# Query products with the masked kv in two 64-feature row tiles, for three of four head groups

## The chip, the cores and the metric

The kernel runs on one core of a Trainium2 chip. The metric is the device time of the whole program in microseconds (us); for the kernel before it is 183.64 us, the median of three runs (183.57 to 183.75). The engines are named as in the profile: PE is TensorE's matmul stream and PEld its weight loads, DVE is VectorE, ACT is ScalarE, POOL is GpSimd, SP is SyncE, which issues most DMAs.

## What is computed

Two blocks read the same layer-normed input of 2048 rows by 512 and are summed with it: a linear attention of 32 heads of 16 features ("A"), and a dense layer with a mish-like activation ("B", 512 to 1792 and back).

```python
def _A_ref(x, wqkv, w_phi, wo):          # x is layer-normed
    q, k, v = heads of x @ wqkv           # 32 heads of 16
    pq, pk = q @ w_phi[h], k @ w_phi[h]
    phi_q = concat([softmax(pq), softmax(-pq)])   # 32 features a head
    phi_k = concat([softmax(pk), softmax(-pk)])
    kv = einsum("bhsf,bhsd->bhfd", phi_k, v)
    z  = einsum("bhsf->bhf", phi_k)
    num = einsum("bhqf,bhfd->bhqd", phi_q, kv)
    den = einsum("bhqf,bhf->bhq", phi_q, z) + 1e-6
    return (num / den, heads joined) @ wo
def _B_ref(x, w1, b1, w2):
    h = x @ w1 + b1
    return (h * tanh(softplus(h))) @ w2
return x + _A_ref(layernorm(x), ...) + _B_ref(layernorm(x), ...)
```

## The kernel before

The 2048 rows are 16 tiles of 128, in four groups of four. The heads stand in four groups `j` of eight, so that one group is 8 x 16 = 128 features wide; `pl` is 0 for the softmax of the logits and 1 for that of their negatives.

**First half.** For each group of rows the kernel computes logits of k (`project`, L156), their exponentials (DVE `extremes`, ACT `exponentials` L228), the softmax (`normalise`), the values (`value`) and, with `accumulate` (L282), kv for all heads in one PSUM tile `pkv`. Between these stand pieces of the hidden layer (`hidden`, L176, each with an ACT mish at L183) as filler for PE. `mask_kv` (L293 to L308, DVE) then copies `pkv` to `kvm`: 128 features by 2 x 4 blocks of 144 columns. A block holds 128 columns of kv, masked so that only the 16 x 16 squares of each head on the diagonal are left, 8 columns of sums of features (the softmax denominators' counterpart to z, from a mask) and 8 columns of the mask itself, written once at the start (L446) from `block`.

**Second half.** The queries go in eight groups `h` of two row tiles. `turn` transposes their exponentials by DMA into `qT` (features on partitions). `attend(h, i)` does one row tile: eight matmuls at L326, each with 128 features of `qT` as weights and 144 columns of `kvm` as the moving side, into a PSUM tile `pnd` of three banks (`blocks`: the first three groups of heads go to bank 0 or 1 by `pl`, the fourth to bank 2). There is one buffer of `pnd`. Four ACT copies empty it: 768 and 256 columns of numerators (L335, L336) and 96 and 32 of denominators (L338, L342, into `ds`). `combine(h)` on DVE makes the factors from `ds` (L358 to L369), scales and adds the two numerators (L376, L383) and issues the DMA that transposes the result (`ob`, L386) from SP's queue. `project_out(h)` (L408) multiplies that with `wo` on top of the second dense layer's sums in `po` (`second_layer`, L399, 14 matmuls a row tile), and `residual` (L416) adds x and writes out.

The order of all this on each engine is written out by hand at the end of the kernel; the framework adds only the waits. Around each `attend` PE runs `second_layer`, `project_out` or `logits`, all of whole 128-row weights, nearly all 512 columns wide. The kernel has one matmul with fewer rows of weights: at L475, near the start, the 14 rows of `b1b` are transposed into `pb`, and as built it is issued on a tile of 32 x 128 of the PE array. All other 1023 recorded matmuls are issued on the whole array of 128 x 128.

Of the kernel before, what the change touches and what calls it, by code (L numbers as in the profile page):

```python
# [8 lines left out]
BF16 = mybir.dt.bfloat16  # L9
FP32 = mybir.dt.float32  # L10

ACT = mybir.ActivationFunctionType
ALU = mybir.AluOpType
# [4 lines left out]
def kernel(  # L18
# [12 lines left out]
    nc = tc.nc  # L31
    P = 128
# [18 lines left out]
    consts = ctx.enter_context(tc.tile_pool(name="consts", bufs=1))  # L51
    wts = ctx.enter_context(tc.tile_pool(name="wts", bufs=1))
    persist = ctx.enter_context(tc.tile_pool(name="persist", bufs=1))
# [4 lines left out]
    opool = ctx.enter_context(tc.tile_pool(name="opool", bufs=2))  # L58
# [3 lines left out]
    x_sb = persist.tile([P, NT, D], BF16, name="x_sb")  # L62
    xnT = persist.tile([P, NT, KT, P], BF16, name="xnT")
    acts = persist.tile([P, FT, S], BF16, name="acts")
    kvm = persist.tile([P, 2, 4, 144], BF16, name="kvm")
    wqk = wts.tile([P, KT, 2 * D], BF16, name="wqk")
    wsrc = wts.tile([P, 4, DH], BF16, name="wsrc")
    wv = wts.tile([P, KT, D], BF16, name="wv")
# [8 lines left out]
    ident = consts.tile([P, P], BF16, name="ident")  # L77
    mhalf = consts.tile([P, TPG], FP32, name="mhalf")
    block = consts.tile([P, 8, 16], BF16, name="block")
    KVmask = consts.tile([P, 136], FP32, name="KVmask")  # L80
    vext = [vpool.tile([P, TPG, 4, 136], BF16, name=f"vext{i}") for i in range(2)]

    ctx.enter_context(tc.manual_schedule())
# [3 lines left out]
    def load_turned(base_col):  # L87

        wT = lnp.tile([P, 4, 512], BF16, name="wT", tag="xn")
        nc.sync.dma_start_transpose(out=wT[:], in_=A_wqkv[:, base_col : base_col + D])  # L90
        return wT
# [96 lines left out]
    p_of, e_of, qT_of = {}, {}, {}  # L188
# [74 lines left out]
    def blocks(kv, pl, j, width):  # L263

        bank, at = (pl, j) if j < 3 else (2, pl)
        return kv[:, bank, at * 144 : at * 144 + width]

    def by_parts(kv, c0, c1):

        v = kv[:, :, 0:432].rearrange("p b (k c) -> p b k c", c=144)  # L270
        return v[:, 0:2, :, c0:c1], v[:, 2, 0:2, c0:c1]
# [17 lines left out]
                    )  # L289

    def mask_kv():
        a, b = by_parts(kv_of[0], 0, 128)
        nc.vector.tensor_tensor(  # L293
            out=kvm[:, :, 0:3, 0:128], in0=a,
            in1=KVmask[:, None, None, 0:128].to_broadcast([P, 2, 3, 128]), op=ALU.mult,
        )
        nc.vector.tensor_tensor(
            out=kvm[:, :, 3, 0:128], in0=b,
            in1=KVmask[:, None, 0:128].to_broadcast([P, 2, 128]), op=ALU.mult,
        )  # L300
        a, b = by_parts(kv_of[0], 128, 129)
        for pl in range(2):
            nc.vector.scalar_tensor_tensor(
                out=kvm[:, pl, 0:3, 128:136], in0=a[:, pl].to_broadcast([P, 3, 8]), scalar=5e-7,
                in1=KVmask[:, None, 128:136].to_broadcast([P, 3, 8]),
                op0=ALU.add, op1=ALU.mult,
            )
        nc.vector.scalar_tensor_tensor(  # L308
            out=kvm[:, :, 3, 128:136], in0=b.to_broadcast([P, 2, 8]), scalar=5e-7,
            in1=KVmask[:, None, 128:136].to_broadcast([P, 2, 8]), op0=ALU.add, op1=ALU.mult,  # L310
        )

    nd_of, oT_of, po_of, tmp_of = {}, {}, {}, {}
# [1 line left out]
    def attend(h, i):  # L315

        if i == 0:
            nd_of[h] = (
                (wkp, wv)[h % 2][:].rearrange("p (i l) c -> p i l c", i=2),
                opool.tile([P, 2, 2, 2, 4, 8], FP32, name="ds"),  # L320
            )
        nm, ds = nd_of[h]
        pnd = ps2.tile([P, 3, 512], FP32, name="pnd", tag="kv")
        for pl in range(2):
            for j in range(4):
                nc.tensor.matmul(  # L326
                    blocks(pnd, pl, j, 144),
                    lhsT=qT_of[h][:, i, pl * 4 + j, :],
                    rhs=kvm[:, pl, j, :],
                    start=True,  # L330
                    stop=True,
                )
        to = nm[:, i, :, :].rearrange("p l (j c) -> p l j c", j=4)
        a, b = by_parts(pnd, 0, 128)
        nc.scalar.copy(to[:, :, 0:3, :], a)  # L335
        nc.scalar.copy(to[:, :, 3, :], b)  # L336
        a, b = by_parts(pnd, 128, 144)
        nc.scalar.copy(  # L338
            ds[:, i, :, :, 0:3, :].rearrange("p l x j h -> p l j x h"),
            a.rearrange("p l j (x h) -> p l j x h", x=2),  # L340
        )
        nc.scalar.copy(ds[:, i, :, :, 3, :], b.rearrange("p l (x h) -> p l x h", x=2))  # L342

    def combine(h, parts=(slice(0, 2),)):

        nm, ds = nd_of.pop(h) if parts[-1].stop == 2 else nd_of[h]
        ds = ds[:].rearrange("p i l x j h -> p i l x (j h)")
        if h not in oT_of:
            ob = lnp.tile([P, 4, 512], BF16, name="ob", tag="xn")
            u = opool.tile([P, 2, 2, 32], FP32, name="u")  # L350
            w = opool.tile([P, 2, 32], FP32, name="w")
            f = opool.tile([P, 2, 2, 32, 2], BF16, name="f")
            tmp_of[h] = ob[:, 0:2, :], u, w, f
            oT_of[h] = ob[:, 2:4, :].rearrange("p i (j c) -> p (i j) c", c=P)
        o_t, u, w, f = tmp_of[h]
        for q in parts:
            n = q.stop - q.start
            nc.vector.tensor_tensor(  # L358
                out=u[:, q], in0=ds[:, q, :, 0, :], in1=ds[:, q, ::-1, 1, :], op=ALU.mult
            )  # L360
            nc.vector.tensor_tensor(
                out=w[:, q], in0=u[:, q, 0, :], in1=u[:, q, 1, :], op=ALU.add
            )
            nc.vector.reciprocal(w[:, q], w[:, q])
            nc.vector.tensor_tensor(
                out=u[:, q], in0=ds[:, q, ::-1, 1, :],
                in1=w[:, q, None, :].to_broadcast([P, n, 2, 32]), op=ALU.mult,
            )
            nc.vector.tensor_copy(  # L369
                f[:, q].rearrange("p i l c o -> p (i l c) o"),  # L370
                u[:, q].rearrange("p i l (c o) -> p (i l c) o", o=1).to_broadcast(
                    [P, n * 64, 2]
                ),
            )
            v = nm[:, q].rearrange("p i l (c e o) -> p (i l c) e o", e=8, o=2)
            nc.vector.tensor_tensor(  # L376
                out=v, in0=v,
                in1=f[:, q].rearrange("p i l c o -> p (i l c) o")[:, :, None, :].to_broadcast(
                    [P, n * 64, 8, 2]
                ),  # L380
                op=ALU.mult,
            )
            nc.vector.tensor_tensor(  # L383
                out=o_t[:, q], in0=nm[:, q, 0, :], in1=nm[:, q, 1, :], op=ALU.add
            )
            nc.sync.dma_start_transpose(  # L386
                out=oT_of[h][:, 4 * q.start : 4 * q.stop, :],
                in_=o_t[:, q].rearrange("p i c -> p (i c)"),
            )
# [51 lines left out]
    nc.gpsimd.memset(mhalf[:], -0.5)  # L441
    for i in range(2):
        nc.gpsimd.memset(vext[i][:, :, :, 128:136], 1.0)
    nc.vector.tensor_copy(KVmask[:, 0:P], block[:].rearrange("p h d -> p (h d)"))
    nc.vector.tensor_copy(KVmask[:, P : P + 8], block[:, :, 0])
    nc.vector.tensor_copy(  # L446
        kvm[:].rearrange("p l j c -> p (l j) c")[:, :, 136:144],
        block[:, None, :, 0].to_broadcast([P, 8, 8]),
    )


    dve, act = nc.vector.tensor_copy, nc.scalar.copy

    warm = ps.tile([P, 4, P], FP32, name="warm", tag="mm")
# [43 lines left out]
    for s in range(NG):  # L498
        exponentials(s, (0, 1) if s else (0,))
        if s > 0:  # L500
            accumulate(s - 1)
        if s < NG:
            for i in range(2 if s else 0):
                value(s * TPG + i, dve)
        if s == 0:
            p_of[1] = smx.tile([P, TPG, 512], BF16, name="p_sb", bufs=1)
            act(p_of[1][:, 0, :], project(wkp, TPG))
            exponentials(0, (1,))
            wide = ps2.tile([P, 3, 512], FP32, name="pwide", tag="kv")
            for i in range(3):  # L510
                project(wkp, TPG + 1 + i, wide[:, i, :])
        else:
            for i in range(TPG):
                logits(s + 1, i, act)
        if 0 < s < NG:
            for i in range(2, TPG):
                value(s * TPG + i, act)
        ln = s + 2 < NG
        if ln:
            t0 = (s + 2) * TPG  # L520
            st = ln_stats(t0, TPG)
            xn = lnp.tile([P, TPG, D], BF16, name="xn", tag="xn")
        elif s == 2:
            wT = load_turned(0)

        normalise(s, 0, (lambda: normal(t0, st, xn)) if ln else None)
        normalise(s, 1)
        if s == 2:
            fold(wT, wqp, ())
        if s == 0:  # L530
            hidden(6)
            act(p_of[1][:, 1:4, :], wide[:])
        hidden((11, 14, 8, 10)[s])
        extremes(s + 1)
# [78 lines left out]
```

## Time and profile before

| what | value |
|---|---|
| median of three runs | 183.64 us (183.57 to 183.75) |
| the profiled execution: its time | 183.6 us |
| its span in the profile | 181.9 us |
| granted TensorE clock | 1.0 in all stretches |
| PE busy | 175.4 us (96%), 1024 matmuls recorded |
| DVE, ACT, POOL busy | 146.5 us (81%), 126.5 us (70%), 25.0 us (14%) |
| L326, `attend`'s matmuls | 128, from 104.1 to 169.2 us |
| matmuls at L399, L408 and L156 (queries) in the second half | fill PE between them |

The span is the time from the first to the last recorded instruction; the 1.7 us between it and the execution's own time lie around it. "Busy" for PE counts modelled ends, so the spacing of starts says more than durations. The chain of waits follows the work that ended last back to its beginning.

### The profile page before, as it was taken

What the parts mean: (1) busy time and instruction counts of PE and PEld (TensorE: products, weight loads), DVE (VectorE), ACT (ScalarE), POOL (GpSimd) and SP (SyncE); (2) the same over time, 40 slices, a digit from 0 to 9 for tenths busy, and PEclk for the clock granted to TensorE, in tenths of its full rate; (3) what the DMA queues carried; (4) which work ended last, traced back from release to release, by engine and by line L of the source; (5) the groups of instructions that cost most, each with busy time, mean ns of one, the idle gap of its engine ahead of it and who ended that gap; (6) DMA issues with size and microseconds to landing.
All of it is one profiled execution on the core that took longest, in us unless ns stands there. A gap on an engine that the chain in (4) does not pass through costs nothing.

```text
span 181.9 us, 2744 instructions
## 1 busy us (share of the span) xinstructions
PE 175.4 (96%) x1024; PEld 90.2 (50%) x1039; DVE 146.5 (81%) x255; ACT 126.5 (70%) x194; POOL 25.0 (14%) x30
## 2 busy tenths in 40 slices
PE   6899999999999999999999999999999999999993
PEld 2454344465444645564465555455554545455561
DVE  2989979986999899988999786399916997647963
ACT  2367999999898899979986989472842558235300
POOL 4403079300793000000000000000000000000000
PEclk9999999999999999999999999999999999999999
DMA  6997796300023600000000840963079302990633
GB/s 145 291 401 267 160 356 175 60 0 5 0 50 65 119 0 0 0 0 4 0 0 0 153 81 10 189 147 63 0 171 203 88 5 41 200 192 31 76 101 115
DMA packets 44393, 18.02 MB, mean 99 GB/s; under 512 B 36828, under 2 KB 43868, under 8 KB 44380
## 3 DMA queue, kind: packets, MB, share of 16 engines
q1 hardware_dynamic: 43408, 17.50, 40.6%
q10 hardware_dynamic: 972, 0.35, 0.7%
q8 instruction: 8, 0.13, 0.3%
q14 instruction: 5, 0.04, 0.1%
HBM read 6.84 MB, written 2.10 MB: 49 GB/s over the span
## 4 chain that ended last, share of the span: by engine, by line
PE 78%; DVE 11%; ACT 4%; DMA 4%; issue 1%; DVEq 0%
PE po L399 22%; PE ph L176 22%; PE pproj L156 17%; PE po L408 7%; PE pkv L282 4%; PE pnd L326 4%; DVE stats L116 4%; ACT e L228 2%; DMA ob<-ob 2%; DMA x_sb<-in_A_x_dram 2%; DVE m L207 2%; DVE xn L128 1%; ACT L183 1%; DVE e L218 1%; DVE wkp L376 1%
## 5 line engine op out<-in xcount | busy, mean ns | idle before, releaser
L399 PE MATMUL po<-w_sb,acts 128*128 128x512 bf16 (+1 forms) x232 | 50.4, 366 | 0.3
L176 PE MATMUL ph<-xnT,w_sb 128*128 128x512 bf16 x224 | 49.5, 379 | 0.4 <-ACT acts L183 0.4
L183 ACT ACTIVATE acts<-ph,b1f 128x512 bf16<-128x512 f32 x56 | 35.2, 703 | 2.8 <-PE ph L176 2.6
L176 PEld LDWEIGHTS <-w_sb 128*128 128x128 bf16 x224 | 21.9, 98 | 26.7 <-issue 0.6
L228 ACT ACTIVATE e<-e 128x2048 bf16<-128x2048 bf16 x16 | 29.8, 1903 | 6.4 <-DVE e L218 6.3
L399 PEld LDWEIGHTS <-acts 128*128 128x128 bf16 x238 | 22.8, 98 | 22.0
L156 PEld LDWEIGHTS <-xnT 128*128 128x128 bf16 x192 | 18.3, 98 | 21.6 <-DMA xnT<-xn 0.8
L194 ACT CAST p_sb<-pproj 128x512 bf16<-128x512 f32 x25 | 13.7, 587 | 9.4 <-PE pproj L156 9.4
L416 DVE TENSOR_TENSOR x_sb<-po,x_sb 128x512 bf16<-128x512 f32 (+1 forms) x17 | 10.6, 655 | 11.4 <-PE po L408 11.4
L246 DVE TENSOR_REDUCE s<-e 128x128 f32<-128x2048 bf16 x8 | 18.2, 2278 | 1.9 <-ACT e L228 1.9
L128 POOL TENSOR_SCALAR xn<-x_sb,mv,rstd 128x512 bf16<-128x512 bf16 x8 | 16.7, 2100 | 0.2
L408 PE MATMUL po<-wqk,ob 128*128 128x512 bf16 (+1 forms) x66 | 14.7, 366 | 0.3 <-DMA ob<-ob 0.2
L156 PE MATMUL pproj<-wv,xnT 128*128 128x512 bf16 x61 | 14.8, 379 | 0.2
L156 PE MATMUL pproj<-wqk,xnT 128*128 128x512 bf16 x62 | 14.4, 379 | 0.1
L335 ACT CAST wkp<-pnd 128x768 bf16<-128x768 f32 x8 | 6.4, 798 | 11.3 <-PE pnd L326 7.4
L207 DVE TENSOR_TENSOR m<-m 128x512 bf16<-128x512 bf16 (+1 forms) x32 | 11.5, 359 | 1.1
L156 PE MATMUL pproj<-wkp,xnT 128*128 128x512 bf16 x50 | 11.8, 379 | 0.1
L207 DVE TENSOR_TENSOR m<-p_sb 128x1024 bf16<-128x1024 bf16 x16 | 11.0, 685 | 1.0 <-ACT p_sb L194 1.0
L326 PEld LDWEIGHTS <-qT 128*128 128x128 bf16 x128 | 9.1, 98 | 3.8
L116 DVE BATCH_NORM_STATS2 stats<-x_sb 128x6 f32<-128x512 bf16 x16 | 10.0, 679 | 1.2 <-DMA x_sb<-in_A_x_dram 1.2
L326 PE MATMUL pnd<-kvm,qT 128*128 128x144 bf16 x128 | 10.6, 226 | 0.0
L259 DVE TENSOR_TENSOR e<-e,r 128x2048 bf16<-128x2048 bf16 x8 | 10.3, 1281 | 0.3
(67 smaller groups left out, 175.2 us busy)
## 6 DMA issues: line engine op xcount, KB each, us to landing
w_sb<-in_B_w_dram SPq DMA_DIRECT2D x2, 1792.0 KB, 8.9
out_dram<-x_sb SPq DMA_DIRECT2D x15, 128.0 KB, 1.9
x_sb<-in_A_x_dram SPq DMA_DIRECT2D x1, 1024.0 KB, 11.7
x_sb<-in_A_x_dram SPq DMA_DIRECT2D x1, 512.0 KB, 4.0
wv<-in_A_wqkv_dram SPq DMA_DIRECT2D x1, 512.0 KB, 4.8
wqk<-in_A_wo_dram SPq DMA_DIRECT2D x1, 512.0 KB
x_sb<-in_A_x_dram SPq DMA_DIRECT2D x1, 256.0 KB, 3.2
x_sb<-in_A_x_dram ACTq DMA_DIRECT2D x1, 256.0 KB, 3.6
```

What stands on the lines that cost most here:

```text
L116: nc.vector.bn_stats(stats[:, i, :], x_sb[:, t0 + i, :])
L128: engine.tensor_scalar(out=xn[:, at + i, :], in0=x_sb[:, t0 + i, :], scalar1=mv[:, i, 0:1], scalar2=rstd[:, i : i + 1], op0=ALU.subtract, ...
L156: nc.tensor.matmul(pp, lhsT=xnT[:, t, kt, :], rhs=w[:, kt, :], start=(kt == 0), stop=(kt == KT - 1),)
L176: nc.tensor.matmul(ph[:], lhsT=w1_sb[:, kt, f * P : (f + 1) * P], rhs=xnT[:, g * TPG : (g + 1) * TPG, kt, :], start=(kt == 0), stop=(kt == ...
L183: nc.scalar.activation(acts[:, f, g * 512 : (g + 1) * 512], ph[:], ACT.Mish, bias=b1f[:, f : f + 1])
L194: copy(p_of[s][:, i, :], pp)
L207: nc.vector.tensor_tensor(out=m[:], in0=src[:, :, 0:half], in1=src[:, :, half : 2 * half], op=op)
L228: nc.scalar.activation(v, v, ACT.Exp)
L246: nc.vector.reduce_sum(t[:], v.rearrange("p t l (c e) -> p (t l c) e", e=16), axis=AX.X)
L326: nc.tensor.matmul(blocks(pnd, pl, j, 144), lhsT=qT_of[h][:, i, pl * 4 + j, :], rhs=kvm[:, pl, j, :], start=True, stop=True,)
L399: nc.tensor.matmul(po[:, c], lhsT=acts[:, f, t * P : (t + 1) * P], rhs=w2_sb[:, f, c], start=(f == 0), stop=False,)
L408: nc.tensor.matmul(po[:, c], lhsT=oT_of[h][:, t % 2 * 4 + j, :], rhs=wo_sb[:, j, c], start=False, stop=(j == 3),)
```

## The change

`attend` splits the products of the first three groups of heads by features. Since `kvm` is block diagonal, the upper 64 features only meet the first 64 of the 128 output columns, and the lower 64 only the last 64. So a block becomes two of 64 features by 72 columns (64 of kv, 4 of sums, 4 of mask), each issued on a row tile of its own, `tile_position` (0, 0) and (64, 0), size 64 x 128, into PSUM bank 0 and bank 1. The fourth group keeps the whole 128 x 144 form, in bank 2, from a tile `kvw`, and is issued first. One `attend` has 2 whole matmuls and 12 on row tiles, in place of 8 whole ones; each still has its own weight load.

`mask_kv` is written for the new layout (7 DVE operations for 5). The three DVE operations at the kernel's start that prepared masks (L444 to L446) go, and a function `masks` does that in nine POOL operations, called in the third round (`s == 2`) of the first half's loop. The ACT copies take the same numbers of columns (768, 256, 96, 32) in another order, and `ds` has another layout, for which `combine` does its products at L358 and L365 once for each row tile.

```diff
-    kvm = persist.tile([P, 2, 4, 144], BF16, name="kvm")
+    kvm = persist.tile([P, 2, 3, 72], BF16, name="kvm")
+    kvw = persist.tile([P, 2, 144], BF16, name="kvw")
...
     def mask_kv():
-        a, b = by_parts(kv_of[0], 0, 128)
-        nc.vector.tensor_tensor(
-            out=kvm[:, :, 0:3, 0:128], in0=a,
-            in1=KVmask[:, None, None, 0:128].to_broadcast([P, 2, 3, 128]), op=ALU.mult,
-        )
...
+        for r in range(2):
+            rows = slice(64 * r, 64 * r + 64)
+            a, b = by_parts(kv_of[0], 64 * r, 64 * r + 64)
+            nc.vector.tensor_tensor(
+                out=kvm[rows, :, :, 0:64], in0=a[rows],
+                in1=KVmask[rows, None, None, 0:64].to_broadcast([64, 2, 3, 64]), op=ALU.mult,
+            )
+            nc.vector.tensor_tensor(
+                out=kvw[rows, :, rows], in0=b[rows],
+                in1=KVmask[rows, None, 0:64].to_broadcast([64, 2, 64]), op=ALU.mult,
+            )
...
+    def masks():
+        nc.gpsimd.memset(kvw[:], 0.0)
+        for r in range(2):
+            rows, own = slice(64 * r, 64 * r + 64), block[64 * r : 64 * r + 64, 4 * r : 4 * r + 4, :]
+            nc.gpsimd.tensor_copy(KVmask[rows, 0:64], own.rearrange("p h d -> p (h d)"))
...
     def attend(h, i):
...
         pnd = ps2.tile([P, 3, 512], FP32, name="pnd", tag="kv")
         for pl in range(2):
-            for j in range(4):
-                nc.tensor.matmul(
-                    blocks(pnd, pl, j, 144),
-                    lhsT=qT_of[h][:, i, pl * 4 + j, :],
-                    rhs=kvm[:, pl, j, :],
-                    start=True,
-                    stop=True,
-                )
+            nc.tensor.matmul(
+                pnd[:, 2, pl * 144 : pl * 144 + 144],
+                lhsT=qT_of[h][:, i, pl * 4 + 3, :],
+                rhs=kvw[:, pl, :],
+                start=True,
+                stop=True,
+            )
+        for pl in range(2):
+            for j in range(3):
+                for r in range(2):
+                    at = pl * 3 + j
+                    nc.tensor.matmul(
+                        pnd[:, r, at * 72 : at * 72 + 72],
+                        lhsT=qT_of[h][64 * r : 64 * r + 64, i, pl * 4 + j, :],
+                        rhs=kvm[64 * r : 64 * r + 64, pl, j, :],
+                        start=True,
+                        stop=True,
+                        tile_position=(64 * r, 0),
+                    )
...
+        a = pnd[:, 0:2, 0:432].rearrange("p r (l j c) -> p r l j c", l=2, j=3)
+        b = pnd[:, 2, 0:288].rearrange("p (l c) -> p l c", l=2)
+        nc.scalar.copy(tr[:, :, :, 0:3, :], a[:, :, :, :, 0:64])
+        nc.scalar.copy(to[:, :, 3, :], b[:, :, 0:128])
+        nc.scalar.copy(dr[:, :, :, 0:3, :], a[:, :, :, :, 64:72])
         nc.scalar.copy(
...
     def combine(h, parts=(slice(0, 2),)):
...
-            nc.vector.tensor_tensor(
-                out=u[:, q], in0=ds[:, q, :, 0, :], in1=ds[:, q, ::-1, 1, :], op=ALU.mult
-            )
...
+            for i in range(n):
+                k = q.start + i
+                nc.vector.tensor_tensor(
+                    out=uh[:, i], in0=ds[:, k, :, 0], in1=ds[:, k, ::-1, 1], op=ALU.mult
+                )
...
-    nc.vector.tensor_copy(KVmask[:, 0:P], block[:].rearrange("p h d -> p (h d)"))
-    nc.vector.tensor_copy(KVmask[:, P : P + 8], block[:, :, 0])
-    nc.vector.tensor_copy(
-        kvm[:].rearrange("p l j c -> p (l j) c")[:, :, 136:144],
-        block[:, None, :, 0].to_broadcast([P, 8, 8]),
-    )
...
         elif s == 2:
             wT = load_turned(0)
+            masks()
```

More of the change, by code (lines that the diff above doesn't have):

```diff
@@ L79 @@
     block = consts.tile([P, 8, 16], BF16, name="block")
-    KVmask = consts.tile([P, 136], FP32, name="KVmask")
+    KVmask = consts.tile([P, 76], FP32, name="KVmask")
     vext = [vpool.tile([P, TPG, 4, 136], BF16, name=f"vext{i}") for i in range(2)]
@@ L291, in mask_kv @@
     def mask_kv():
-        a, b = by_parts(kv_of[0], 0, 128)
-        nc.vector.tensor_tensor(
-            out=kvm[:, :, 0:3, 0:128], in0=a,
-            in1=KVmask[:, None, None, 0:128].to_broadcast([P, 2, 3, 128]), op=ALU.mult,
-        )
-        nc.vector.tensor_tensor(
-            out=kvm[:, :, 3, 0:128], in0=b,
-            in1=KVmask[:, None, 0:128].to_broadcast([P, 2, 128]), op=ALU.mult,
-        )
+        for r in range(2):
[9 more added lines that the diff above has]
+            )
         a, b = by_parts(kv_of[0], 128, 129)
@@ L303, in mask_kv @@
             nc.vector.scalar_tensor_tensor(
-                out=kvm[:, pl, 0:3, 128:136], in0=a[:, pl].to_broadcast([P, 3, 8]), scalar=5e-7,
-                in1=KVmask[:, None, 128:136].to_broadcast([P, 3, 8]),
+                out=kvm[:, pl, :, 64:68], in0=a[:, pl].to_broadcast([P, 3, 4]), scalar=5e-7,
+                in1=KVmask[:, None, 64:68].to_broadcast([P, 3, 4]),
                 op0=ALU.add, op1=ALU.mult,
@@ L308, in mask_kv @@
         nc.vector.scalar_tensor_tensor(
-            out=kvm[:, :, 3, 128:136], in0=b.to_broadcast([P, 2, 8]), scalar=5e-7,
-            in1=KVmask[:, None, 128:136].to_broadcast([P, 2, 8]), op0=ALU.add, op1=ALU.mult,
+            out=kvw[:, :, 128:136], in0=b.to_broadcast([P, 2, 8]), scalar=5e-7,
+            in1=KVmask[:, None, 68:76].to_broadcast([P, 2, 8]), op0=ALU.add, op1=ALU.mult,
+        )
[4 more added lines that the diff above has]
+            nc.gpsimd.tensor_copy(KVmask[rows, 0:64], own.rearrange("p h d -> p (h d)"))
+            nc.gpsimd.tensor_copy(KVmask[rows, 64:68], own[:, :, 0])
+            nc.gpsimd.tensor_copy(
+                kvm[rows].rearrange("p l j c -> p (l j) c")[:, :, 68:72],
+                own[:, None, :, 0].to_broadcast([64, 6, 4]),
+            )
+        nc.gpsimd.tensor_copy(KVmask[:, 68:76], block[:, :, 0])
+        nc.gpsimd.tensor_copy(
+            kvw[:, :, 136:144], block[:, None, :, 0].to_broadcast([P, 2, 8])
         )
@@ L319, in attend @@
                 (wkp, wv)[h % 2][:].rearrange("p (i l) c -> p i l c", i=2),
-                opool.tile([P, 2, 2, 2, 4, 8], FP32, name="ds"),
+                opool.tile([P, 2, 2, 4, 2, 8], FP32, name="ds"),
             )
@@ L324, in attend @@
         for pl in range(2):
-            for j in range(4):
-                nc.tensor.matmul(
-                    blocks(pnd, pl, j, 144),
-                    lhsT=qT_of[h][:, i, pl * 4 + j, :],
-                    rhs=kvm[:, pl, j, :],
-                    start=True,
-                    stop=True,
-                )
-        to = nm[:, i, :, :].rearrange("p l (j c) -> p l j c", j=4)
-        a, b = by_parts(pnd, 0, 128)
-        nc.scalar.copy(to[:, :, 0:3, :], a)
-        nc.scalar.copy(to[:, :, 3, :], b)
@@ L337, in attend @@
-        a, b = by_parts(pnd, 128, 144)
+            nc.tensor.matmul(
[16 more added lines that the diff above has]
+                        tile_position=(64 * r, 0),
+                    )
@@ new lines, in attend @@
+        to = nm[:, i, :, :].rearrange("p l (j c) -> p l j c", j=4)
+        tr = to.rearrange("p l j (r c) -> p r l j c", r=2)
+        dr = ds[:, i].rearrange("p l j r c -> p r l j c")
+        a = pnd[:, 0:2, 0:432].rearrange("p r (l j c) -> p r l j c", l=2, j=3)
[3 more added lines that the diff above has]
+        nc.scalar.copy(dr[:, :, :, 0:3, :], a[:, :, :, :, 64:72])
@@ L338, in attend @@
         nc.scalar.copy(
-            ds[:, i, :, :, 0:3, :].rearrange("p l x j h -> p l j x h"),
-            a.rearrange("p l j (x h) -> p l j x h", x=2),
+            ds[:, i, :, 3, :, :].rearrange("p l r (x h) -> p l x r h", x=2),
+            b[:, :, 128:144].rearrange("p l (x r h) -> p l x r h", x=2, r=2),
         )
-        nc.scalar.copy(ds[:, i, :, :, 3, :], b.rearrange("p l (x h) -> p l x h", x=2))
     def combine(h, parts=(slice(0, 2),)):
         nm, ds = nd_of.pop(h) if parts[-1].stop == 2 else nd_of[h]
-        ds = ds[:].rearrange("p i l x j h -> p i l x (j h)")
+        ds = ds[:].rearrange("p i l j r (x h) -> p i l x (j r) h", x=2)
@@ L357, in combine @@
             n = q.stop - q.start
-            nc.vector.tensor_tensor(
-                out=u[:, q], in0=ds[:, q, :, 0, :], in1=ds[:, q, ::-1, 1, :], op=ALU.mult
-            )
+            uh = u[:, q].rearrange("p i l (c h) -> p i l c h", h=4)
+            wh = w[:, q, None, :].to_broadcast([P, n, 2, 32]).rearrange(
+                "p i l (c h) -> p i l c h", h=4
+            )
+            for i in range(n):
+                k = q.start + i
+                nc.vector.tensor_tensor(
+                    out=uh[:, i], in0=ds[:, k, :, 0], in1=ds[:, k, ::-1, 1], op=ALU.mult
+                )
             nc.vector.tensor_tensor(
@@ L364, in combine @@
             nc.vector.reciprocal(w[:, q], w[:, q])
-            nc.vector.tensor_tensor(
-                out=u[:, q], in0=ds[:, q, ::-1, 1, :],
-                in1=w[:, q, None, :].to_broadcast([P, n, 2, 32]), op=ALU.mult,
-            )
+            for i in range(n):
+                k = q.start + i
+                nc.vector.tensor_tensor(
+                    out=uh[:, i], in0=ds[:, k, ::-1, 1], in1=wh[:, i], op=ALU.mult
+                )
             nc.vector.tensor_copy(
@@ L443 @@
         nc.gpsimd.memset(vext[i][:, :, :, 128:136], 1.0)
-    nc.vector.tensor_copy(KVmask[:, 0:P], block[:].rearrange("p h d -> p (h d)"))
-    nc.vector.tensor_copy(KVmask[:, P : P + 8], block[:, :, 0])
-    nc.vector.tensor_copy(
-        kvm[:].rearrange("p l j c -> p (l j) c")[:, :, 136:144],
-        block[:, None, :, 0].to_broadcast([P, 8, 8]),
-    )
     dve, act = nc.vector.tensor_copy, nc.scalar.copy
```

## The prediction

> **What bounds the kernel.** I read the page's busy shares first, then its chain of waits, then the chain in order of time around `attend`, then the records of PE and PEld one by one where row sizes change.
>
> ```profile
> PE 175.4 (96%) x1024; PEld 90.2 (50%) x1039; DVE 146.5 (81%) x255; ACT 126.5 (70%) x194; POOL 25.0 (14%) x30
> ...
> PE 78%; DVE 11%; ACT 4%; DMA 4%; issue 1%; DVEq 0%
> ```
>
> PE is the bound. The 11% of DVE and 4% of DMA in the chain lie before 29 us, in the last microsecond of PE's output and in one stretch from 108.4 to 115.5 us; elsewhere in the half where `attend` stands, PE runs without a gap. The chain in order of time shows it:
>
> ```profile
> 127.90 1.73 PE po L408 x8
> 129.63 0.50 PE pnd L326 x8
> 130.13 1.08 PE po L399 x5
> ```
>
> So an `attend` holds PE for 0.50 us, and what it takes more or less moves the end by as much, 16 times, except where something else is late. The one such place is the first `project_out`, in the timeline of all engines:
>
> ```profile
> 114.69 0.66 PE L326 MATMUL pnd<-kvm,qT 128*128 128x144 bf16 x8
> ...
> 115.50 1.41 PEld L408 LDWEIGHTS <-ob 128*128 128x128 bf16 x8 [0.34 <-DMA ob<-ob]
> ```
>
> The last of these eight matmuls starts at 115.128 in the records, the next at 115.506: 378 ns instead of 63, so PE waits 0.315 us for the transpose of `combine(0)`'s result.
>
> **What one matmul costs.** Starts in a row are 216 ns apart at 512 columns (L399), 55.6 at 128 (L98) and 62.5 at 144 (L326). That is 0.418 ns a column and some 2 ns on top, so 72 columns would take 32.5 ns and 14 columns 8 ns alone. Weight loads are not what spaces L326 today: at 6.67 us, where PE starts from rest, two loads start 15 ns apart, and a load of 98 ns lies under the matmul before it. The first matmul behind a fresh load is 11 ns late (229 against 219 ns at L98, and 66 to the next start instead of 55.6).
>
> **What a change of tile size costs.** The kernel has one case: `pb` (L475), 14 rows, issued on a 32 x 128 tile, between whole-array matmuls.
>
> ```profile
> 8.52 0.38 PE L140 MATMUL ptr<-ident,xn 128*128 128x128 bf16 x4 [0.55 <-DVE wkp L106]
> 8.85 0.16 PE L475 MATMUL pb<-ident,b1b 14*128 14x14 bf16 x1
> 8.95 1.04 PE L156 MATMUL pproj<-wkp,xnT 128*128 128x512 bf16 x4
> ```
>
> ```profile
> 8.52 0.21 PEld L140 LDWEIGHTS <-xn 128*128 128x128 bf16 x3 [0.53 <-issue]
> 8.83 0.09 PEld L475 LDWEIGHTS <-b1b 14*128 14x128 bf16 x1
> 8.94 0.55 PEld L156 LDWEIGHTS <-xnT 128*128 128x128 bf16 x4
> ```
>
> Everywhere else a load starts 1 to 2 ns after the start of the matmul before it. Here `pb`'s load comes at 8.833, 147 ns after the last transpose began (8.686), though its DMA had landed by 6.22. The next load comes 92 ns after `pb` began (8.851 to 8.943), and it waits for nothing. The matmuls before them stream for 53 and 6 ns, so each change of size held the next load for 94 and 86 ns beyond the stream. From transposes to `pproj` without a change of size (10.21 us) the spacing is the usual 56. I take these two rows as the price, with 15 ns from load to matmul (4 ns in the records and the 11 above). The Trainium skill, TensorEngine Tiling (Array Packing), Key Properties, says that changing the tiling mode drains the TensorE, and that changing the tile alone does not; it gives no figure. Rows and rule agree on the first half; the second no row here shows, and it is a rival below.
>
> **The change on PE, step by step.** From the first whole matmul of an `attend` to the first matmul behind it:
> - whole to whole: 62.5 ns.
> - second whole to first row tile, a change of size: 60 stream + 94 + 15 = 169 ns.
> - eleven steps p between the twelve row-tile matmuls.
> - last row tile to the next whole matmul, a change back: 30 stream + 86 + 15 = 131 ns.
>
> Sum 362.5 + 11p, against 500 now: d = 11p - 137.5 ns for each `attend`. No row shows two tiles at work side by side, so p is bounded. Lower end 16.25: two streams of 32.5 ns run wholly beside each other, and two loads 15 ns apart just fit. Upper end 32.5: the tiles run one after the other. Beyond that, 55.6 is the closest spacing that the trace sustains. The rows nearest to alternating tiles are the stream (32.5) and a late first matmul (11): I take a pair at 32.5 + 11 = 43.5, p = 21.75, one load in each pair not hidden. Then d = +102 ns; at the ends +41 and +220. (The Trainium skill, TensorE: Matmul & The Clock Gate, in its section on 56 against 53.3 ns, gives about 25 ns as the least distance of starts, measured there without tiles; by it d = 137.5 ns and the time 185.6.)
>
> **The first four `attend`s** lie before the wait at 115.5. PE's own work now reaches it 0.315 us early, and after the change 4d - 0.315 late. The waited-for chain starts at the end of the second `attend`, so it moves by 2d, and by what `combine(0)` gains: at L358 and L365 two products of 64 columns for one of 128. DVE's independent operations follow each other at column time plus some 65 ns (256 columns at L297 in 331, 24 at L303 in 90), so a 64-column one adds 0.13 us, and the second's 0.25 to its successor (L358 at 168.49 to L361 at 168.74) replaces 0.325: +0.055, twice, 0.11 us. The shift there is the larger of 4d - 0.315 and 2d + 0.11: 0.31 us at d = 102.
>
> **What lies beside other work.**
> - ACT's copies keep their columns. Their spacing is 0.695, 0.264, 0.131 us for 768, 256, 96 columns: about 0.84 ns a column and 48 ns, though L338 reads runs of 8 columns and L336 of 128. Shorter runs cost nothing there; I count nothing. The cover is thin: the copies of `attend(7, 0)` end at 168.32, and `attend(7, 1)` starts at 168.50, so copies 0.2 us longer would stop PE there.
> - `combine`'s other 0.11 us: results land early (`combine(7)`'s last transpose at 177.19, its first use at about 177.88), and the parts of `combine(7)` have no added operation.
> - `mask_kv`: 2 x (400 + 65) + 2 x (133 + 65) ns by the same rule, 1.33 us for 1.20, and three small ones as before. It ends at 99.3 and is first used at 104.1; behind it on DVE three copies of logits wait, which PE needs again at 102.56 at the earliest. Nothing.
> - `masks` on POOL: nine operations of 0.1 to 0.4 us by POOL's rows at the start, after POOL's last work (56.4 us) and over 40 us before their use. SP's and POOL's queues carry nothing else then that they would hold up. DVE loses three operations at 2.4 to 2.8 us, while it waits for x until 3.98. Nothing.
>
> **Sum**, against the profiled execution's 183.6 us (span 181.9 and 1.7 around it; the median of 183.64 is the same for this purpose): 0.31 + 12 x 0.102 = +1.5 us, **185.1 us**. At p = 16.25: 0.19 + 0.49 = +0.7, 184.3. At p = 32.5: 0.57 + 2.64 = +3.2, 186.8.
>
> **Rivals.**
> - *Changes of size are cheap in this form, the pairs run side by side* (ends faster). For it: the price rests on one small matmul with another tile size, at the start of the kernel. Against: it shows twice, in and out, alike to 8 ns. Without the price an `attend` takes 157.5 + 11p: at p = 16.25 that is 164 ns less than now; the first four then give 2 x -0.164 + 0.11 = -0.22, the twelve -1.97, 181.4 us. At p = 21.75 it is 182.3. It decides from the point where both changes together cost less than 342 - 11p, 103 to 163 ns, where the rows say 205.
> - *The tiles do not overlap and loads do not hide*: p between 32.5 and 55.6. For it: each small matmul has a load that now has 30 ns of cover in place of 60. At 55.6 d = 474 ns, first four 1.58, twelve 5.69, 190.9 us.
> - *Each change between the two tiles costs what a change of size does*: p = 131, d = 1.30 us, 4.9 + 15.6 = +20.5, 204 us. Nothing in the profile excludes it; the rule above speaks against it.
> - *The change doesn't do what it says*: as built, 96 matmuls stand on tile (0, 0) and 96 on (64, 0), each 64 rows by 128, with waits only at the first whole matmul of an `attend`. That leaves nothing for this rival.
>
> **Chances.** Forecast with its price of 205 ns and p from 16.25 to 32.5: 0.63, its own range 184.3 to 186.8. First rival, 181.4 to 184.3: 0.22. Second, above 186.8: 0.12. Third: 0.03. The range of 182.2 to 187.3 leaves out some 0.06 below and 0.12 above. A difference of 0.2% (0.37 us) is about what a measurement of this kernel can tell from none. Faster by more takes 0.18 of the first rival; within it lie the other 0.04 of it and 0.03 of the forecast's low end; slower 0.75.
>
> **What would show it.** In the profile after, the load behind the second whole matmul of each `attend`, and that of the matmul behind the last row tile, should start some 150 and 115 ns after the matmul before them; starts of row-tile matmuls should average 22 ns, in unequal steps; the span from an `attend` to the next work should be about 0.60 us for 0.50; the wait at the first `project_out` should be 0.2 us. If the loads follow at once at the changes of size, the first rival holds; if row-tile starts are 33 ns or more apart, the second. ACT copies over 0.75 us at the 768 columns would prove my zero for ACT wrong.

## The result, and the profile after

The changed kernel takes **184.96 us** (median of four, 184.93 to 185.07) against 183.69 us (183.57 to 184.05) for the kernel before beside it: a ratio of 1.0066, with a 95% interval of 1.0051 to 1.0081, so 0.66% or 1.2 us slower. The forecast was 185.1, slower. The size came out, but not from the terms that the forecast summed. These are the busy shares, the queues and the chain on the page of the changed kernel:

```profile
span 183.1 us, 2959 instructions
PE 175.0 (96%) x1119; PEld 87.6 (48%) x1135; DVE 147.6 (81%) x268; ACT 126.4 (69%) x194; POOL 28.5 (16%) x39
...
q8 instruction: 9, 0.15, 0.3%
...
PE 10%; DMA 3%; DVE 1%; DVEq 0%; issue 0%
```

The chain no longer reaches back to the start: it begins at a DMA. The chain in order of time names it, with start and length in us:

```profile
155.47 4.82 DMA qT<-e
160.29 0.04 issue
160.34 0.30 PE pnd L343 x2
160.64 0.30 PE pnd L354 x12
160.94 0.32 PE po L437
```

PE waits for the transposed queries of `attend(6, 0)`, which it did not before. The rest of that `attend` is what the forecast spoke of. Here is one without a wait, at 129.66 us, in the timeline of PE (start, length to the last modelled end, count):

```profile
129.66 0.29 PE L343 MATMUL pnd<-kvw,qT 128*128 128x144 bf16 x2
129.88 0.37 PE L354 MATMUL pnd<-kvm,qT 64*128 64x72 bf16 x12
130.18 0.60 PE L437 MATMUL po<-w_sb,acts 128*128 128x512 bf16 x2
```

From 129.66 to 130.18 it is 0.52 us, against 0.50 before. To the nanosecond, the records give these distances from start to start in the `attend`s without a wait: 62 or 63 between the wholes, 158 or 159 to the first row tile, then 3 or 4 and 29 to 36 in turn (173 or 174 for eleven steps, 15.7 on average), and 127 or 128 back to the whole array; the matmul behind has its successor after 226 instead of 216. So an `attend` costs 521 to 523 and some 10 behind it, against 500: **33 ns more**. The wait at the first `project_out` is shorter, 0.11 us from start to start for 0.315, where the forecast had 0.2 (the load at L446, 0.17 us of idle, where it was 0.34):

```profile
115.63 0.33 PEld L446 LDWEIGHTS <-ob 128*128 128x128 bf16 x3 [0.17 <-DMA ob<-ob]
115.64 0.60 PE L446 MATMUL po<-wqk,ob 128*128 128x512 bf16 x2
```

The shift of each `attend` against the kernel before adds up like this: +0.21 us at the first one (104.337 for 104.125), 16 x 0.033 = +0.53, -0.21 at that `project_out`, and +0.72 at `attend(6, 0)`, whose first matmul starts 938 ns after the one before it instead of 216. The sum is 1.25, the spans differ by 183.1 - 181.9 = 1.2. Of the first 0.21, 0.17 is there at 6.8 us already, when the first transposed weights land; the other 0.05 comes near 84.6 us, and its cause is open.

What made the transpose late? It is issued at 155.47 and lands at 160.29, 4.8 us; before it was issued at 154.94 and landed at 158.16, 3.2 us. The stretches of the changed kernel (columns: length, then PE, PEld, DVE, ACT, POOL busy, clock, DMA share, GB/s; the DMA share is the packets' own time against that of 16 engines and can pass 1) show the DMA engines almost still while transposes are under way:

```profile
157.00:158.00 1.00, 1.00 (x6) 0.49 (x5) 0.93 (x4) 0.00 (x0) 0.00 (x0) 1.00 1.04 190
158.00:159.00 1.00, 1.00 (x7) 0.42 (x5) 0.97 (x2) 0.00 (x0) 0.00 (x0) 1.00 2.33 147
159.00:160.00 1.00, 0.78 (x4) 0.16 (x2) 0.96 (x3) 0.00 (x0) 0.00 (x0) 1.00 0.11 15
160.00:161.00 1.00, 0.66 (x15) 0.47 (x16) 1.00 (x3) 0.00 (x0) 0.00 (x0) 1.00 1.28 286
```

15 GB/s for a microsecond. The kernel before, while it transposes the same queries, stays at 181 and 182:

```profile
157.00:158.00 1.00, 0.95 (x6) 0.45 (x5) 0.90 (x4) 0.00 (x0) 0.00 (x0) 1.00 0.98 181
158.00:159.00 1.00, 1.00 (x6) 0.42 (x5) 1.00 (x1) 0.00 (x0) 0.00 (x0) 1.00 1.00 182
```

At 158.22 a single packet of 16,384 bytes on queue 8, "instruction", begins and takes 0.88 us. From one such packet to the next the records have on average 127 matmuls and 128 loads of PE in the kernel before (125 and 127 in the changed one), so they fit a fetch for each 256 or so of PE's instructions. The change adds 192 instructions; there is a ninth packet, and the later ones come at other places. My theory after the result was that this fetch, not the row tiles, holds up the transposes and costs 0.72 us. The rivals: SP's queue issues the transposes later (0.53 us later than before), or something of the row tiles slows the DMAs.

### The profile page after: what moved, and what is told of

It reads as the page before. It is cut to its first block, busy times and chain, and to the rows that moved or that the text cites. A ratio compares the mean times of both kernels' runs of the same rounds, so it can differ in the third digit from the quotient of the medians.

```text
span 183.1 us, 2959 instructions
## 1 busy us (share of the span) xinstructions
PE 175.0 (96%) x1119; PEld 87.6 (48%) x1135; DVE 147.6 (81%) x268; ACT 126.4 (69%) x194; POOL 28.5 (16%) x39
## 5 line engine op out<-in xcount | busy, mean ns | idle before, releaser
L437 PEld LDWEIGHTS <-acts 128*128 128x128 bf16 x238 | 22.1, 98 | 22.8
L446 PE MATMUL po<-wqk,ob 128*128 128x512 bf16 (+1 forms) x66 | 14.5, 366 | 0.3 <-PE pnd L354 0.2
L367 ACT CAST wv<-pnd 128x768 bf16<-128x768 f32 x8 | 6.3, 792 | 5.8 <-PE pnd L354 3.6
L219 DVE TENSOR_TENSOR e<-m,p_sb 128x2048 bf16<-128x2048 bf16 x8 | 9.8, 1226 | 0.3
```

The costliest lines, as they stand in the source:

```text
L367: nc.scalar.copy(tr[:, :, :, 0:3, :], a[:, :, :, :, 0:64])
L437: nc.tensor.matmul(po[:, c], lhsT=acts[:, f, t * P : (t + 1) * P], rhs=w2_sb[:, f, c], start=(f == 0), stop=False,)
L446: nc.tensor.matmul(po[:, c], lhsT=oT_of[h][:, t % 2 * 4 + j, :], rhs=wo_sb[:, j, c], start=False, stop=(j == 3),)
```

## Experiments

**The kernel before, again.** No edit; a second profile, for the 0.17 us at the start.

> The kernel before, unchanged, for a second profile. In the profile of the changed kernel the first transposed weights (wT) land 0.16 us later than in that of the kernel before (6.79 against 6.63 us) and everything behind them starts 0.17 us later. Theory A: that is scatter of one DMA from execution to execution; here the landing may then lie anywhere from 6.6 to 6.8 us and the first attend begins as much later as it. Theory B: it comes from the change (three DVE operations less at the start); then this profile shows 6.63 us again, within 0.03. On either the time is 183.6 to 183.8 us, and the first query transpose of attend(6, 0) takes about 3.2 us from issue to landing.

184.25 us in its one run (183.76, 183.63 to 183.91, in the ten others of the same kernel beside it). The first load of transposed weights comes at 7.31 us, against 6.67 in the first profile, and the first `attend` 0.646 us later (104.771). From there on every distance is the same, and the transpose takes 3.2 us. So the start scatters with the landing of one DMA, by more than theory A allowed. The 0.17 us of the changed kernel's profile can't be put down to the change: in the five profiles of the changed kernel and its variants PE is 0.12 to 0.23 us late at 8.9 us, and in the two others of the kernel before, this one and the one with a longer warm-up below, 0.65 and 0.12. The first profile is the early one.

**Fetches moved away, changed kernel.**

```diff
-    for _ in range(12):
+    for _ in range(48):
         nc.tensor.matmul(
-            warm[:], lhsT=ident[:], rhs=ident[:, None, :].to_broadcast([P, 4, P]),
+            warm[:, 0, 0:128], lhsT=ident[:], rhs=ident[:, 0:128],
```

> The changed kernel with 36 more matmuls (and weight loads) in the warm-up, as many columns in all as before, so that PE's instruction fetches (one 16 KB packet for each 256 instructions) come 72 instructions earlier in the work: at about 153 us in place of 158.2. Theory A, the fetch that coincides with the query transposes for attend(6, 0) delays them by 1.6 us and makes PE wait 0.72 us there: the transpose takes about 3.2 us for 4.8, the wait is gone and the time falls by 0.7, to 184.2 us. Theory B, the transposes are late since they are issued 0.53 us later, behind the outputs in SP's queue: the wait stays and the time is 184.9 us. On both an attend holds PE for 0.033 us more than before.

184.26 us, ratio to the kernel before 1.0030 (1.0018 to 1.0043): 0.7 us less than the changed kernel. The fetch comes at 152.55 us. The transpose is issued at 155.55, later than ever, and lands at 158.78, 3.2 us. The same stretches as above:

```profile
157.00:158.00 1.00, 1.00 (x7) 0.42 (x5) 0.93 (x4) 0.00 (x0) 0.00 (x0) 1.00 1.09 205
158.00:159.00 1.00, 1.00 (x6) 0.46 (x5) 0.97 (x2) 0.00 (x0) 0.00 (x0) 1.00 0.97 188
159.00:160.00 1.00, 1.00 (x12) 0.48 (x12) 0.97 (x2) 0.00 (x0) 0.00 (x0) 1.00 0.95 185
```

188 and 185 GB/s in place of 147 and 15, and PE has no gap. The later issue is excluded as the cause. The fetches still meet transposes: the one at 117.57 us falls on query transposes too, and the first of them takes 4.85 us; it lands at 119.94 us, the next `attend` begins at 120.91, and PE doesn't wait. What is left of the change is 0.55 us (0.33 to 0.79): 16 x 0.033 less the 0.2 at the first `project_out`, and some 0.2 that would fit the scatter of the start (0.23 in this profile).

**Fetch moved onto the transposes, kernel before.** No row tiles; the warm-up as above, with 89 matmuls of 69 columns.

> The kernel before with 77 more matmuls (and weight loads) in the warm-up, as many columns in all, so that the fetch that comes at 169.4 us now comes at about 157.7, while the first query transpose for attend(6, 0) is under way; no row tiles anywhere. Theory A (fetch against transposes): that transpose lands 1.6 us later, at 159.8 us, where attend(6, 0) would begin at 159.2, so PE waits some 0.6 us and the time is 184.2 to 184.3 us. Theory B (it is the later issue, or something of the row tiles): no wait, 183.65 us.

185.57 us, ratio 1.0103 (1.0089 to 1.0117): 1.8 us more, not 0.6. The chain in order of time has two DMAs in it, and PE's waits have a third place:

```profile
155.72 4.81 DMA qT<-e
160.54 0.05 issue
160.58 0.67 PE pnd L326 x8
...
176.12 3.37 DMA ob<-ob
```

```profile
PEld L408 <- DMA ob<-ob: 1.8, 2, 1.0
...
PEld L326 <- DMA qT<-e: 0.9, 1, 0.9
```

The fetch came at 158.47, and the transpose took 4.81 us again; `attend(6, 0)` begins 0.58 us late, as expected. I had looked at one fetch only. The one at 113.15 meets the transpose for the first `project_out`: 3.85 us from issue (112.38) to landing (116.23) in place of 3.21, and 0.66 us more of waiting there. The one at 176.55 meets the kernel's last transpose, and the last eight matmuls begin 721 ns after the one before them instead of 216, 0.5 us late. With 0.12 us at the start the three waits (0.66, 0.59 and 0.5) make up the difference of the spans, 183.7 - 181.9. So the same work on PE, with idle matmuls at the start that end when they did before, is 1% slower by the place of three fetches.

**Half products on the whole array.** The twelve half products keep their 72 columns and their banks, but use all 128 rows, the other 64 zero.

```diff
-                        lhsT=qT_of[h][64 * r : 64 * r + 64, i, pl * 4 + j, :],
-                        rhs=kvm[64 * r : 64 * r + 64, pl, j, :],
+                        lhsT=qT_of[h][:, i, pl * 4 + j, :],
+                        rhs=kvm[:, pl, j, r, :],
                         start=True,
                         stop=True,
-                        tile_position=(64 * r, 0),
```

> The changed kernel with its 12 half products in an attend issued on the whole array: 128 rows of weights, 72 columns, the other half of the moving side zero. No changes of tile size and nothing side by side, the same number of PE instructions. From the spacing of starts (32.5 ns for 72 columns, 62.5 for 144) an attend takes 2 x 62.5 + 12 x 32.5 = 515 ns, 18 less than with row tiles (533) and 15 more than before. Theory A (the fetch, whose place depends on the number of instructions alone): the wait before attend(6, 0) stays, 0.6 to 0.8 us, and the time is 184.6 to 184.7 us. Theory B (the row tiles make the transposes late): the wait is gone, 183.9 us. If PE can't go below some 55 ns a matmul with its own load, an attend takes 0.79 us and the time is near 189 us.

185.11 us, ratio 1.0073 (1.0061 to 1.0086). PE at the same `attend`, from 129.72 to 130.24:

```profile
129.72 0.29 PE L346 MATMUL pnd<-kvw,qT 128*128 128x144 bf16 x2
129.85 0.55 PE L357 MATMUL pnd<-kvm,qT 128*128 128x72 bf16 x12
130.24 0.60 PE L439 MATMUL po<-w_sb,acts 128*128 128x512 bf16 x2
```

It takes 513 ns, with 32 to 33 between starts: each with its own load, one after the other. That is less than on row tiles (521, and 11 behind). The wait at `attend(6, 0)` is there without any row tile, 0.82 us from start to start, with the fetch at 158.23 and the landing at 160.35:

```profile
160.39 0.11 PEld L346 LDWEIGHTS <-qT 128*128 128x128 bf16 x2 [1.15 <-DMA qT<-e]
```

The row tiles are excluded as its cause. The time is 0.4 to 0.5 us above what I expected. In the records the 16 shorter `attend`s save 0.27 us against row tiles, but the wait at the first `project_out` grows by 0.15 and this one by 0.1, so the spans are equal (183.1 both); the 0.15 us between the medians lies outside the span.

**Four changes of tile size in an `attend`.** With the warm-up of the second experiment; the order is whole, six halves, whole, six halves.

> The changed kernel with the longer warm-up of x1_after_fetch_moved (184.26 us, no late transpose), and in each attend the order whole, six half products, whole, six half products: four changes of tile size for two, nothing else. Theory A (each change holds PE for the streaming to end and some 90 ns more): in the trace of the changed kernel the start behind a change comes after 158 and 128 ns, where it would be 62 and 29 without, so two more cost 96 + 99 = 195 ns an attend: 717 ns for 522, 16 times 3.1 us, 187.4 us (0.7 more if a fetch meets a transpose again, since all moves). Theory B (the pause belongs to the first row-tile load of an attend, or to the wait of its first matmul, and not to the change): 522 ns and 184.3 us.

187.34 us, ratio 1.0197 (1.0182 to 1.0212); 187.4 was expected. One `attend`, from 130.79 to 131.52:

```profile
130.79 0.23 PE L343 MATMUL pnd<-kvw,qT 128*128 128x144 bf16 x1
130.95 0.27 PE L353 MATMUL pnd<-kvm,qT 64*128 64x72 bf16 x6
131.15 0.24 PE L343 MATMUL pnd<-kvw,qT 128*128 128x144 bf16 x1
131.32 0.27 PE L353 MATMUL pnd<-kvm,qT 64*128 64x72 bf16 x6
131.52 0.61 PE L436 MATMUL po<-w_sb,acts 128*128 128x512 bf16 x2
```

734 ns, 212 more than with two changes (195 expected); the steps are 159, 128, 168 and 127 at the changes. 16 x 0.212 = 3.4 us, less what the wait at the first `project_out` takes up (0.14 us are left of it with two changes, nothing with four), and 187.34 - 184.26 = 3.1: the price belongs to the change of size, each time it is made.

**One tile after the other.** Same warm-up; six halves on tile (0, 0), then six on (64, 0).

> The changed kernel with the longer warm-up of x1_after_fetch_moved, and the twelve half products of an attend in the order six on tile (0, 0), then six on tile (64, 0), for alternating ones; as many changes of size as before. Theory A (alternating tiles run side by side, each matmul still streams its 72 columns): starts within a tile are 30 to 33 ns apart, the second tile may start beside the first only once, an attend takes 62 + 158 + 10 x 32 + 4 + 128 = 0.67 us for 0.52, and the time is 184.26 + 16 x 0.15 = 186.7 us. Theory B (row-tile matmuls are short whatever their order: 16.5 ns each): 0.52 us and 184.3 us.

185.19 us, ratio 1.0076 (1.0059 to 1.0093). One `attend` begins at 130.04; its half products and the work behind it:

```profile
130.26 0.45 PE L354 MATMUL pnd<-kvm,qT 64*128 64x72 bf16 x12
130.64 0.60 PE L437 MATMUL po<-w_sb,acts 128*128 128x512 bf16 x2
```

From its beginning to 130.64 it is 600 ns: between the theories, close to neither. In the records of the first `attend` the twelve starts are 39, 34, 9, 24, 14, 18, 16, 17, 16, 32, 33 ns apart. The records don't name the tile. But read as two rows of six, one for each tile and the second 82 ns behind the first, they are 39, 34, 33, 32 and 33 apart on the first tile and 38, 34, 33, 32 and 33 on the second. So a row-tile matmul does stream its 72 columns, as theory A has it, and tiles overlap where both have work; but the second tile begins beside the first far earlier than I supposed, so that only about three matmuls at each end stand alone.

## Why the prediction was right, and where it was not

- *A change of size holds the next load for 94 and 86 ns beyond the stream.* Right, from one 14-row matmul. It is 158 ns in (169 forecast) in all 16 `attend`s, and 128 out with 10 or 11 behind (131 forecast) in the 12 where the next record is there and PE doesn't wait; four changes cost twice as much. The rule of the Trainium skill (TensorEngine Tiling (Array Packing), Key Properties) holds in both halves: a change of size drains, and between the two tiles starts are 3 to 4 ns apart. With that the first and the third rival fall; the second falls with p.
- *p = 21.75 ns.* The term that was mis-sized. It is 15.7, a little below my lower end of 16.25: loads are wholly hidden, and a pair needs 32 ns. With 15.7 the forecast's own formula, 362.5 + 11p, gives 535 where 532 was measured. d is 33 ns, not 102, and the 16 `attend`s cost 0.53 us, not 1.6.
- *The first four move the first `project_out` by 2d + 0.11.* Wrong in sign: that chain comes 0.08 us earlier against the first `attend`. The change back to whole weights lies behind the last half product, so ACT doesn't wait for it; in the records that last matmul starts 394 ns into an `attend` for 437 before. That makes 0.04 of the 0.08. And the split product at L395 costs `combine` nothing there: its first half needs only the first row tile's `ds` and starts at 108.32, before ACT has finished the second's. From the second half to the DMA it is 3.81 us for 3.86, though the split at L404 adds 0.07.
- *What lies beside other work costs nothing.* ACT's copies of 768 columns took 804 ns at most (800 before). The forecast's sign of error, copies over 0.75 us, was badly set, since they took 0.80 before; the spacing to the next copy, 0.696 us behind the second `attend`, is the same in both kernels. `masks` ended at 60.1 us, and PE has no further gap in the second half.
- *The sum.* Without late transposes the forecast's terms, rightly sized, give 0.53 - 0.2 = +0.3 us; the experiment with the fetch moved away measured 0.55 (0.33 to 0.79). The other 0.7 us came from a mechanism that no step or rival had: the count of PE's instructions. I noted 96 more matmuls and loads, priced their time on PE and did not ask what else instructions cost. The profile of the kernel before showed it: eight packets of "instruction" on queue 8, one of them at 169.41 us in the trace's DMA records, where a transpose of `ob` took 2.5 us to issue for the usual 1.2. So the time was right by luck, by errors that nearly cancel: by the forecast's own formula p made it 1.0 us too much and the term at the first `project_out` another 0.25, while 0.7 for the fetch and 0.2 of a later start were missing. Of the 1.2 us that were measured, only some 0.3 come from the mechanism that was forecast.

None of the kernels here is faster than the one before. By an estimate from these distances, without the changes of size an `attend` on row tiles would take 2 x 62.5 + 173 + 30 = 328 ns for 500, 172 saved; the two changes cost 205. Two row tiles of queries behind one pair of changes would then save 2 x 172 - 205 = 139 ns in place of losing 33 each, but need a second `pnd` of three PSUM banks, beside the three of the first and the five buffers of `po` and the projections. That wasn't tried.

## What to carry to other kernels

A tile of the PE array pays when the matmuls between two changes of tile size save more than both changes cost, here some 200 ns; count the changes, not only the matmuls. When an edit changes the number of instructions, look where the instruction fetches fall, and which DMA transposes are then under way with little slack. A step of a few tenths of a per cent in a kernel with unchanged work may be just that; here idle instructions in the warm-up moved it.

## What the runs showed of the hardware that was not expected

**An instruction fetch holds up DMA transposes.** Three profiles have a 16 KB fetch during the transposes for `attend(6, 0)`, at 158.22, 158.47 and 158.23 us: the first of these transposes takes 4.8 to 4.9 us from issue to landing. In the five others it takes 3.2. The rest of the query transposes say the same: in all eight profiles, the 20 with a recorded landing where a fetch begins between 0.4 us before and 2.8 us after the issue take 3.7 to 4.9 us, the 84 others 3.1 to 3.5. In the changed kernel's records the packets of 256 bytes, some 21 ns each otherwise, take 191 and 352 ns on average in the two quarters of a microsecond from 158.5 on, and then few come until 159.9, although the fetch ended at 159.1. Why they stay away that long is open. The Trainium skill, Runtime: NRT & Kernel Launch, Instruction fetch mechanics, says that instructions come in 16 KiB blocks of 256 through a DMA queue of the sequencer's own, and that the cost is "mostly hidden". The traces agree with the blocks: packets of 16,384 bytes on a queue of their own, one for some 255 recorded matmuls and loads. PE's own stream runs on through the fetches of the second half, so there the cost is hidden; for transposes under way it was 1.6 us, and 0.5 to 0.8 us of the kernel's time at each place without slack.

**Alternating tiles start almost together.** Their loads start 4 ns apart as well (129.877 and 129.881 us for the first pair of the `attend` shown), and the loads of the next pair come 11 ns later (129.892 and 129.896), while the first pair's 72 columns, some 30 ns, are still streaming.
